# Attention and two feed-forward layers on one core: side work given out one operation at a time, weights converted during layer one, sums in two tiles

## The chip, the cores and the metric

The kernel runs on one core of a Trainium2 chip. A core has a matrix engine (TensorE, PE in the profile), a vector engine (VectorE, DVE), a scalar engine (ScalarE, ACT), GpSimd (POOL) and a sync engine (SP), which here issues nearly all DMAs. Each engine runs its own instructions in order; engines wait for each other through semaphores. The metric is the device time of one launch in microseconds (us).

## The reference

Three functions follow one another, all on 6016 tokens of 256 channels in float32.

```python
qn = q / (np.linalg.norm(q, axis=1, keepdims=True) + 1e-06)      # over the 6016 tokens
kn = k / (np.linalg.norm(k, axis=1, keepdims=True) + 1e-06)
s = kn.transpose(0, 2, 1) @ qn / tau                             # 256 x 256
a = softmax(s);  x = v @ a                                       # 6016 x 256

xn = x / np.sqrt(np.mean(x * x, axis=-1) + 1e-06) * rms_g        # layer one
g = xn @ w_gate;  val = xn @ w_val                               # 256 -> 1536
y = (silu(g) * val) @ w_out                                      # 1536 -> 256

h = y @ w_in                                                     # layer two, 256 -> 2048
out = (h - np.tanh(h)) @ w_out2                                  # 2048 -> 256
```

The weights of both layers are float64 in memory.

## The kernel before

**Numbers.** A float32 factor is split into a high part, rounded to the format in which TensorE takes one pass (`hi_of`, a ScalarE copy), and the rest (`lo_of`, a VectorE subtraction). A product is then three matmuls (`prod`, L132): high with high, low weight with high, high weight with low. The float64 weights are converted by integer operations: one ScalarE copy that scales the upper word (L249, L1010) and three VectorE operations (shift, sign, bits: L253, L256, L260).

**Stages.** Tokens stand in 12 blocks of 512 (the first two 512 and 384), two blocks a pair. (1) Attention reads q and k, accumulates the 256 x 256 scores and the norms, and makes the matrix a. (2) Pair 0 of layer one goes block by block in `gate_block` (L935), while the `converter` turns layer one's weights into high and low parts and saves them to DRAM. (3) Pairs 1 to 5 of layer one use a scheme with 7 products in place of 8 for a 2 x 2 block product. A pair has 6 units (`first_unit`, L799), each with a gate half and a value half; a half is one call of `unit` (L749) with 7 products of 3 matmuls each and 4 fillers. A filler (`fill`) is one product of the second matrix (`acc`), 3 matmuls, of values that an earlier unit left. (4) Layer two runs pairs 0 to 5 with 8 units each (`second_unit`, L1106): 7 products and 8 fillers, 45 matmuls. Pair 0 of layer two has two halves of 448 columns, all others 512.

**A unit.** `unit` uses four PSUM banks X, T, Y, Z. It forms X and T, copies X to Y and T to m5 (ScalarE), adds a product to Y, makes Z = Y + m5 (VectorE), and goes on in X, Y, Z and Y. After each quarter a hook takes a result out: c11 from X, c22 from Y + m5, c12 from Z, c21 from Y. The gate half applies silu; the value half multiplies and splits into `uc` and `ulc`, which the fillers use. What is left over at a unit's end is put in `carried` and runs in the next unit's hooks `early` and `next`.

**Side work.** Everything that is not on this path is a generator wrapped in `Work` (L35), which yields after one operation or a few. `side(n)` (L157) does up to n steps: at each one `Work.clock` goes up, and the first work in the list that can go on takes a step, whatever engine it is for. A yielded number waits for so many clocks, a function until it is true, and "pe" until `between` (L165) between two halves. `force` (L172) and `finish` (L984) run a work's steps one after another until a condition holds. The side works are:
- `first_sums` (L343): the sums of layer one's weights that the scheme needs, six of them, from DRAM into the tile `wraw`;
- `x_operands` (L632): the operands of the next pair. It splits two blocks of v, multiplies by a (x, 12 matmuls a block), squares, takes the mean over channels by a matmul (`ms`), computes 1/rms in a narrow tile with two DRAM trips (`row` to m, `back` to `rs`), multiplies, and then `operands` (L588) forms and splits seven sums;
- `second_weights` (L996): conversion of layer two's weights, 16 items, each loaded into `wraw` (512 KB) and saved to DRAM. At the start of pair 5 `finish(w2_work)` (L1094) runs what is left;
- `second_sums` (L1026): eight times, loads the saved weights into `wraw`, splits them, forms four sums and splits these. It starts when the unit of pair 5 whose weights it replaces is over. `force(s2_work, ...)` (L1182) runs what a unit of layer two still lacks;
- `y_operands` (L1062): in layer two, loads y and forms the operands of the next pair.

## Time and profile before

The median of three runs is 1309.99 us (1307.97 to 1310.6). The profiled execution took 1313.08 us; its span, from the first to the last instruction, is 1311.3 us, and its mean granted TensorE clock 0.95.

| engine | busy, us | share of the span | instructions |
|---|---|---|---|
| TensorE, matmuls | 1175.4 | 90% | 4988 |
| TensorE, weight loads | 943.3 | 72% | 4988 |
| VectorE | 832.9 | 64% | 1402 |
| ScalarE | 690.0 | 53% | 1219 |

Busy time is the sum over the engine's instructions; weight loads overlap matmuls, and the ends of matmuls are modelled. "Idle before" in a row is the time in which the engine had nothing to do before that instruction, and the arrow names what ended it. The clock in a window is the share of full speed that TensorE was granted.

### The profile page before, as it was taken

Reading aid. Unit: us, or ns where it says so; the run is one execution under the profiler, and the core shown is the slowest. Engines: PE = TensorE matmul, PEld = TensorE weight load, DVE = VectorE, ACT = ScalarE, POOL = GpSimd, SP = SyncE. Lnnn points to the kernel's source line nnn. Section 1 sums busy time; section 2 is a strip of 40 time slices with the busy share of each in tenths; the row PEclk is TensorE's granted clock in tenths of the full one; section 3 lists DMA queues with packets and bytes.
Section 4 is the critical chain, followed back from the end, with each engine's and each line's share of the span. In section 5 each row is a group of like instructions: output and inputs, shape, how many; then the busy total and the mean of one; then the engine's idle time right before and its main releaser. Section 6 shows DMA issues by size and latency. Waiting matters only on the chain.

```text
span 1311.3 us, 13924 instructions
## 1 busy us (share of the span) xinstructions
PE 1175.4 (90%) x4988; PEld 943.3 (72%) x4988; DVE 832.9 (64%) x1402; ACT 690.0 (53%) x1219; POOL 0.7 (0%) x6
## 2 busy tenths in 40 slices
PE   9688979995998999999619998879999999999998
PEld 8567867774776777777418777667888888878887
DVE  5777556646556566655636666667667676676765
ACT  5454535554544654654315455446565565665655
POOL 0000000000000000000000000000000000000000
PEclk9788989997999999999859998889999999999999
DMA  9443121102101201111041002101010010100000
GB/s 365 155 160 127 33 65 60 49 4 69 57 25 57 73 25 57 64 33 41 24 132 49 17 23 90 32 25 53 9 51 15 9 49 8 41 17 1 33 0 33
DMA packets 37737, 73.05 MB, mean 56 GB/s; under 512 B 6426, under 2 KB 8218, under 8 KB 37668
## 3 DMA queue, kind: packets, MB, share of 16 engines
q1 hardware_dynamic: 37380, 71.12, 16.0%
q10 hardware_dynamic: 288, 1.05, 0.2%
q8 instruction: 39, 0.64, 0.2%
q14 instruction: 30, 0.25, 0.1%
HBM read 52.45 MB, written 19.70 MB: 55 GB/s over the span
## 4 chain that ended last, share of the span: by engine, by line
PE 55%; DVE 10%; ACT 8%; DMA 3%; issue 2%; SPq 0%; ACTq 0%; DVEq 0%
PE acc L136 23%; PE Yh L136 8%; PE Xh L136 4%; PE Yv L136 4%; PE Yg L136 3%; PE Zh L136 2%; PE Th L136 2%; PE Xv L136 2%; DMA rs<-back 1%; PE Xg L136 1%; ACT hc L124 1%; PE Zv L136 1%; DVE ulc L130 1%; PE x L136 1%; PE Tv L136 1%
## 5 line engine op out<-in xcount | busy, mean ns | idle before, releaser
L136 PE MATMUL acc<-hc,l 128*128 128x512 f32 (+1 forms) x768 | 236.5, 389 | 0.0
L130 DVE TENSOR_TENSOR lc<-wc,hc 128x512 fp32r<-128x512 f32 (+1 forms) x192 | 127.3, 677 | 82.4 <-ACT hc L124 82.4
L136 PEld LDWEIGHTS acc<-hc,l 128*128 128x128 f32 x768 | 146.7, 191 | 27.8
L124 ACT ACTIVATE hc<-wc 128x512 fp32r<-128x512 f32 (+1 forms) x192 | 113.8, 617 | 83.6 <-DVE wc L1114 83.6
L124 ACT ACTIVATE uc<-t 128x512 fp32r<-128x512 f32 x120 | 72.3, 626 | 148.9 <-DVE t L779 148.9
L136 PE MATMUL acc<-lc,l 128*128 128x512 f32 (+1 forms) x384 | 149.1, 388 | 0.0
L130 DVE TENSOR_TENSOR ulc<-t,uc 128x512 fp32r<-128x512 f32 x120 | 79.7, 685 | 12.6 <-ACT uc L124 12.1
L136 PEld LDWEIGHTS acc<-lc,l 128*128 128x128 f32 x384 | 73.2, 191 | 13.7
L136 PE MATMUL Yg<-T2h,sh 128*128 128x512 f32 x30 | 13.3, 444 | 47.7 <-ACT Yg L127 47.5
L1114 DVE TENSOR_TENSOR wc<-Yh,wc 128x512 f32<-128x512 f32 (+1 forms) x48 | 32.7, 680 | 30.8 <-ACT wc L1111 30.8
L1111 ACT ACTIVATE wc<-Xh 128x512 f32<-128x512 f32 (+1 forms) x48 | 28.2, 588 | 44.6 <-PE Xh L136 44.6
L747 DVE TENSOR_TENSOR Zg<-Yg,m5g 128x512 f32<-128x512 f32 x30 | 20.9, 698 | 45.4 <-PE Yg L136 29.5
L782 ACT ACTIVATE t<-t 128x512 f32<-128x512 f32 x30 | 19.0, 632 | 58.0 <-DVE t L747 53.1
L747 DVE TENSOR_TENSOR s<-Yh,m5h 128x512 f32<-128x512 f32 (+1 forms) x48 | 32.6, 680 | 25.5 <-PE Yh L136 25.5
L1111 ACT ACTIVATE wc<-Yh 128x512 f32<-128x512 f32 (+1 forms) x48 | 28.2, 589 | 37.9 <-PE Yh L136 37.9
L408 PE MATMUL S<-q,k 128*128 128x256 f32 x188 | 44.3, 398 | 1.5 <-DMA k<-k_in 1.5
L136 PEld LDWEIGHTS Yg<-T2h,sh 128*128 128x128 f32 x30 | 5.7, 189 | 55.5 <-ACT Yg L127 54.3
L408 PEld LDWEIGHTS S<-q,k 128*128 128x128 f32 x188 | 37.3, 201 | 7.8 <-issue 1.2
L1111 ACT ACTIVATE wc<-s 128x512 f32<-128x512 f32 (+1 forms) x48 | 30.0, 624 | 23.9 <-DVE s L747 23.8
L136 PE MATMUL Th<-T1h,l2s 128*128 128x512 f32 (+1 forms) x96 | 33.3, 422 | 8.8 <-ACT l2s L124 8.3
L1114 DVE TENSOR_TENSOR wc<-Xh,wc 128x512 f32<-128x512 f32 (+1 forms) x48 | 32.5, 676 | 8.8 <-ACT wc L1111 8.4
L136 PE MATMUL Xh<-B11h,l 128*128 128x512 f32 (+1 forms) x96 | 31.1, 396 | 7.7 <-ACT l L124 6.1
(684 smaller groups left out, 3008.7 us busy)
## 6 DMA issues: line engine op xcount, KB each, us to landing
q<-q_in SPq DMA_DIRECT2D x11, 512.0 KB
vraw<-vT_in SPq DMA_DIRECT2D x11, 512.0 KB
y<-r SPq DMA_DIRECT2D x22, 256.0 KB
y<-y SPq DMA_DIRECT2D x20, 256.0 KB
outT<-r SPq DMA_DIRECT2D x20, 256.0 KB
k<-k_in SPq DMA_DIRECT2D x9, 512.0 KB
raw<-w_in_in SPq DMA_DIRECT2D x8, 512.0 KB
l<-y SPq DMA_DIRECT2D x16, 256.0 KB
```

The source lines that it names most:

```text
L124: nc.scalar.activation(out=dst, in_=src, func=AF.Copy, scale=scale)
L130: nc.vector.tensor_sub(out=dst, in0=src, in1=f32(hi))
L136: nc.tensor.matmul(out, a, b, start=start and i == 0, stop=i == 2, skip_group_check=True)
L408: nc.tensor.matmul(S[m][:, :C], kt[:, j, m * P:(m + 1) * P], qt[:, j, :], start=(i == 0 and j == 0), stop=(i == NCH - 1 and j == chunks[i] ...
L747: nc.vector.tensor_add(out=o, in0=a, in1=b)
L782: nc.scalar.activation(out=o, in_=a, func=AF.Silu)
L1111: nc.scalar.activation(out=t[c][:, :n], in_=src, func=AF.Tanh)
L1114: nc.vector.tensor_sub(out=t[c][:, :n], in0=src, in1=t[c][:, :n])
```

## The change

`Work` now says what its next operation is for: "A" (ScalarE), "D" (VectorE) or "pe". `side(a, d)` raises the clock once and gives out up to d VectorE and then up to a ScalarE operations, each to the first work that has one of that kind; a work that has just had a ScalarE operation gets its VectorE operation at a later clock. The table SIDE fixes the numbers at each hook of a unit: 9 and 9 in a unit of layer one, 3 and 3 in one of layer two. `urgent` holds copies out of PSUM that `hurry` puts behind a unit's first two copies.

In `x_operands`, x of pair 1 comes from unsplit v and a in full precision, the low part of v is one operation of 1024 elements, and the two trips of 1/rms through DRAM are issued without clocks between them. `operands` splits two sums at a time. In a unit of layer one the product for c22 and the low part of c21 move from the next gate half's start to the end of the value half, and the high part of c12 the other way; silu of c22 goes behind that of c12. In layer two the low part of c22 moves from `early` to `next`.

`finish(w2_work)` is gone; the conversion of layer two's weights stands behind x in the list in all pairs of layer one, and waits 2 clocks instead of 6 for a load. `second_sums` becomes two works, for the even units in the tile `wraw` and the odd ones in `vraw`; each splits 1024 elements in one operation and loads its next tile right behind its last operation. The core of the diff:

```diff
-SIDES = ((1, 2), (1, 2))
+SIDES = (((1, 1), (1, 2)), ((1, 1), (1, 2)))
...
     def __init__(self, steps):
-        self.steps, self.pe, self.ready, self.done = steps, False, None, False
-
-    def run(self):
+        self.steps, self.kind, self.ready, self.done, self.acted = steps, None, None, False, -1
+        self.advance()
+
+    def advance(self):
         got = next(self.steps, self)
-        self.pe, self.ready = got == "pe", None
+        self.kind = self.ready = None
         if got is self:
             self.done = True
...
-        return not self.done and not self.pe and (self.ready is None or self.ready())
+        else:
+            self.kind = got
+
+    def can(self, kind):
+        while self.ready and self.ready():
+            self.advance()
+        return self.kind == kind and (kind == "A" or self.acted < Work.clock)
+
+    def run(self):
+        if self.kind == "A":
+            self.acted = Work.clock
+        self.advance()
 
...
-    def side(count=1):
-        for _ in range(count):
-            Work.clock += 1
-            w = next((w for w in works if w.can()), None)
-            if w:
-                w.run()
+    def side(a=0, d=0):
+
+        Work.clock += 1
+        for kind, count in (("D", d), ("A", a)):
+            for _ in range(count):
+                w = next((w for w in works if w.can(kind)), None)
+                if w:
+                    w.run()
         works[:] = [w for w in works if not w.done]
...
-        w = next((w for w in works if w.pe), None)
+        w = next((w for w in works if w.can("pe")), None)
         if w:
-            w.pe = False
             w.run()
 
     def force(w, until):
         while not until():
             assert not w.done
             w.run()
+            hurry()
...
-            yield 3
-            for _ in block_sums(y):
-                yield
+            yield 2
+            yield from block_sums(y)
...
+        def split(*parts):
+            hs = []
+            for nm, t in parts:
+                yield "A"
+                hs.append(oh(f"{nm}h"))
+                hi_of(hs[-1][:, :n], t[:, :n])
+            for (nm, t), h in zip(parts, hs):
+                yield "D"
+                l = ol(f"{nm}l")
+                lo_of(l[:, :n], t[:, :n], h[:, :n])
+                out[nm] = (h[:, :n], l[:, :n])
...
+        yield from split(("T1", t1), ("T2", t2))
+        yield "D"
         sub(b12, b22, b12)
-        yield
-        yield from split("T2", t2)
+        yield "D"
         sub(t2, b21, t2)
         yield lambda: last() > 0
-        yield from split("B21", b21)
-        yield from split("T3", b12)
+        yield from split(("B21", b21), ("T3", b12))
         yield lambda: last() > 1
-        yield from split("B22", b22)
-        yield from split("T4", t2)
+        yield from split(("B22", b22), ("T4", t2))
...
-        for t in range(2):
-            b = 2 * p + t
-            if b not in v_raw:
-                load_v(b)
-                yield 4
-            raw = v_raw.pop(b)
-            vh, vl = (act_tile(f"v{x}", 1, f"v{x}{b}", shape=V2) for x in "hl")
+        b0 = 2 * p
+        split, sqs, parts = {}, [[], []], {}
+
+        def split_v(t):
+            raw = v_raw.pop(b0 + t)
+            if p == 1:
+                split[t] = raw
+                return
+            vh, vl = (act_tile(f"v{x}", 1, f"v{x}{b0 + t}", shape=V2) for x in "hl")
             for kk in range(KC):
+                yield "A"
                 hi_of(vh[:, kk], raw[:, kk])
-                yield
-                lo_of(vl[:, kk], raw[:, kk], vh[:, kk])
...
+            yield "D"
+            lo_of(vl, raw, vh)
+            split[t] = vh, vl
+            if b0 + t + 1 < len(blocks):
+                load_v(b0 + t + 1)
...
+                    if p == 1:
+                        x_matmul_full(o, b0 + t, c, kk, split[t])
+                    else:
+                        vh, vl = split[t]
+                        prod(o, a_hl[kk][c], (vh[:, kk], vl[:, kk]), kk == 0)
+                if c == 0:
+                    x_out(t, c, o)
+                else:
+                    urgent.append(lambda: x_out(t, c, o))
...
+        def mean_square(t, later):
+            o = take(f"ms{b0 + t}", 1)
+            for i, x in enumerate(parts[t]):
+                nc.tensor.matmul(o, mean, x, start=i == 0, stop=i == 1)
+
+            def out():
+                copy(sqs[t][1][:1, :], o[:1, :])
+                nc.sync.dma_start(out=row[t:t + 1, :], in_=sqs[t][1][:1, :])
+
+            if later:
+                urgent.append(out)
+            else:
+                out()
+
+        if b0 not in v_raw:
+            load_v(b0)
+            yield 3
+        yield from split_v(0)
+        yield "pe"
+        x_products(0)
+        if p == 1:
+            load_v(b0 + 1)
+        yield from split_v(1)
+        yield from squares(0)
+        yield "pe"
+        mean_square(0, False)
+        x_products(1)
+        if p == 1:
+            load_v(b0 + 2)
+        yield 2
+        yield from squares(1)
+        yield "pe"
+        mean_square(1, True)
+        yield 1
...
-        yield 5
+        yield 4
+        yield "D"
         nc.vector.tensor_scalar_add(out=m, in0=m, scalar1=1e-6)
         for i, op in enumerate(rsqrt_ops(m, y, s)):
+            if i % 3 == 1:
+                yield "D"
             op()
-            if i % 3 == 0:
-                yield
         nc.sync.dma_start(
             out=back.rearrange("t (p g) -> p t g", g=NG), in_=y.rearrange("p (t g) -> p t g", t=2))
-        yield 5
         rs = []
         for t in range(2):
             rs.append(sq_tile(f"rs{p}_{t}"))
             nc.sync.dma_start(out=rs[t], in_=back[t:t + 1, :].to_broadcast([P, BLK]))
-        yield 5
+        yield 4
         for t in range(2):
             for c in range(KC):
+                yield "D"
                 x = B[KC * t + c]
                 nc.vector.tensor_mul(out=x, in0=x, in1=rs[t])
-                yield
...
+        hurry()
...
-            side(2)
+            side(*SIDE["g11"])
 
         def g22(Y, m5):
             t["c22"] = ut(f"t22_{i}")
             add(t["c22"][:, :n], Y, m5)
-            gate("c22", t["c22"][:, :n])
+            side(*SIDE["g22"])
 
         def g12(Z):
             t["c12"] = ut(f"t12_{i}")
             gate("c12", Z)
+            gate("c22", t["c22"][:, :n])
+            side(*SIDE["g12"])
...
-            side(3)
+            side(*SIDE["g21"])
...
+            side(*SIDE["v11"])
...
+            side(*SIDE["v12"])
...
-            high("c12")
+            value("c22", sums["c22"])
+            lower("c21")
 
             def later():
-                lower("c21")
-                value("c22", sums["c22"])
+                high("c12")
                 high("c22")
...
-        between()
-        unit(unit1[i][0], x, n, GAPS1, dict(early=carry(0), next=carry(1), c11=g11, c22=g22, c12=g12, c21=g21),
-             f"g{i}")
-        between()
-
         def early():
             place[1] = (i, 1)
-            side(4)
-
+            side(*SIDE["early"])
+
+        unit(unit1[i][0], x, n, GAPS1, dict(early=carry(0), next=carry(1), c11=g11, c22=g22,
+             c12=g12, c21=g21), f"g{i}")
+        between()
         unit(unit1[i][1], x, n, GAPS1,
-             dict(early=early, next=lambda: None, c11=v11, c22=v22, c12=v12, c21=v21), f"v{i}")
+             dict(early=early, next=lambda: side(*SIDE["next"]), c11=v11, c22=v22, c12=v12, c21=v21), f"v{i}")
         place[1] = (i, 2)
-        side(1)
+
+
+    SIDE = dict(
+        g11=(2, 1), g22=(0, 2), g12=(1, 2), g21=(1, 2), early=(2, 2), next=(0, 0), v11=(2, 0),
+        v12=(1, 0), h_early=(1, 1), h11=(1, 1), h12=(0, 0), h21=(1, 1))
 
...
-                yield 6
+                yield 2
+                yield "A"
                 y = act_tile("wy", 1, f"y{j}{x}", F32, [P, 2 * C])
                 nc.scalar.activation(
                     out=y, in_=raw[:, :, 1].bitcast(F32), func=AF.Copy, scale=REBIAS)
-                yield
+                yield "D"
                 shift(y.bitcast(I32))
-                yield
+                yield "D"
                 sign(y.bitcast(I32), raw[:, :, 1])
-                yield
+                yield "D"
                 bits(y.bitcast(I32), raw[:, :, 0])
                 nc.sync.dma_start(out=saved2[j][x], in_=y)
...
-    def second_sums():
-        for j in range(NU2):
...
-            y = act_tile("wraw", 1, f"l2y{j}", F32, [P, 1, 4 * C])
+    def second_sums(first, tag):
+
+        yield lambda: w2_work.done and place[0] >= NP - 1
+
+        def load(j):
+            y = act_tile(tag, 1, f"l2y{j}", F32, [P, 1, 4 * C])
             for x in range(2):
                 nc.sync.dma_start(out=y[:, 0, 2 * C * x:2 * C * (x + 1)], in_=saved2[j][x])
-            yield 4
-            hs = []
-            for x, tag in enumerate((ta, tb)):
-                t = wpool.tile([P, 4 * C], F32R, tag=tag, name=f"l2{j}{x}")
-                hs.append((t[:, :2 * C], t[:, 2 * C:]))
-                hi_of(hs[x][0], y[:, 0, 2 * C * x:2 * C * (x + 1)])
-                yield
-                lo_of(hs[x][1], y[:, 0, 2 * C * x:2 * C * (x + 1)], hs[x][0])
-                yield
-            for _ in block_sums(y):
-                yield
+            return y
+
+        for j in range(first, NU2, 2):
+            ta, tb, ts, free = HOMES[j]
+            y = load(j)
+            yield 2
+            yield lambda free=free: place[0] > NP - 1 or (
+                place[1][0] > free or place[1] == (free, 2))
+            h, l = (wpool.tile([P, 4 * C], F32R, tag=tag, name=f"l2{j}{x}")
+                    for x, tag in (("h", ta), ("l", tb)))
+            yield "A"
+            hi_of(h, y[:, 0])
+            yield "D"
+            lo_of(l, y[:, 0], h)
+            yield from block_sums(y)
             t = late[0].tile([P, 2 * 3 * P], F32R, tag=ts, name=f"l2s{j}")
             sh, sl = t[:, :3 * P], t[:, 3 * P:]
-            h, l = hs[0]
+            yield "A"
             hi_of(sh, y[:, 0, P:4 * P])
-            yield
+            yield "A"
             hi_of(h[:, :P], y[:, 0, :P])
+            yield "D"
             lo_of(sl, y[:, 0, P:4 * P], sh)
-            yield
+            yield "D"
             lo_of(l[:, :P], y[:, 0, :P], h[:, :P])
-            unit2[j], out2[j] = seven(h, l, sh, sl), hs[1]
-            yield
+            unit2[j], out2[j] = seven(h, l, sh, sl), (h[:, 2 * C:], l[:, 2 * C:])
...
-        yield 5
+        yield 2
...
     w2_work = Work(second_weights())
-    s2_work = Work(second_sums())
+    s2_works = [Work(second_sums(i, tag)) for i, tag in enumerate(("wraw", "vraw"))]
...
         else:
-            finish(w2_work)
             x_work = Work(y_operands(0, progress(p, NU1), x_next))
-        works[:] = ([sums_work] if not sums_work.done else []) + [x_work]
-        works.append(w2_work if p + 1 < NP else s2_work)
+        works[:] = [w for w in (sums_work, x_work, w2_work, *s2_works) if not w.done]
...
-            side(1)
+            side(*SIDE["h11"])
...
             def later():
                 lower("c12")
                 high("c22")
-                lower("c22")
 
             carried[0].append(later)
-            side(1)
+            carried[1].append(lambda: lower("c22"))
+            side(*SIDE["h21"])
...
-            side(2)
+            side(*SIDE["h_early"])
...
         for j in range(NU2):
-            force(s2_work, lambda: unit2[j] is not None)
+            force(s2_works[j % 2], lambda: unit2[j] is not None)
             second_unit(j, x, n, A)
```

## Rows read from the trace of the kernel before

**Rows 1.** Table of windows, by stage: us, busy (instructions) by engine, clock, DMA share, GB/s.
```profile
185.20:193.48 8.28, 1.57 (x6) 1.06 (x5) 4.67 (x10) 1.52 (x3) 0.00 (x0) 0.78 0.39 128
193.48:205.93 12.45, 10.39 (x35) 7.80 (x33) 9.25 (x17) 6.55 (x12) 0.00 (x0) 0.73 0.00 1
205.93:310.45 104.52, 91.90 (x393) 71.91 (x392) 61.40 (x111) 51.27 (x94) 0.00 (x0) 0.96 0.16 52
310.45:423.27 112.82, 103.75 (x424) 79.07 (x425) 70.63 (x122) 56.13 (x101) 0.00 (x0) 0.97 0.14 45
423.27:532.37 109.10, 101.67 (x425) 79.41 (x424) 67.11 (x116) 56.39 (x102) 0.00 (x0) 0.98 0.15 46
641.44:690.51 49.07, 10.66 (x35) 8.20 (x33) 19.09 (x32) 11.78 (x21) 0.00 (x0) 0.58 0.32 104
690.51:775.75 85.24, 84.36 (x364) 67.30 (x363) 53.15 (x91) 43.51 (x81) 0.00 (x0) 1.00 0.09 32
775.75:885.18 109.43, 90.66 (x361) 74.97 (x360) 70.08 (x136) 55.25 (x112) 0.00 (x0) 0.88 0.14 46
969.93:1053.09 83.16, 82.59 (x362) 67.12 (x361) 58.59 (x91) 51.43 (x92) 0.00 (x0) 1.00 0.08 26
```

**Rows 2.** Table of windows, single half-units of layer one and units of layer two.
```profile
490.40:497.88 7.48, 7.48 (x34) 6.20 (x33) 3.89 (x8) 1.99 (x4) 0.00 (x0) 1.00 0.04 2
373.51:381.15 7.64, 7.64 (x34) 6.04 (x33) 5.86 (x17) 4.71 (x9) 0.00 (x0) 1.00 0.18 43
532.37:544.22 11.85, 9.48 (x34) 7.03 (x33) 8.72 (x15) 8.23 (x16) 0.00 (x0) 0.86 0.00 1
554.75:564.20 9.45, 8.66 (x36) 6.35 (x35) 3.79 (x6) 5.63 (x11) 0.00 (x0) 1.00 0.33 112
506.55:515.90 9.35, 7.80 (x34) 6.12 (x33) 4.25 (x7) 1.98 (x4) 0.00 (x0) 1.00 0.63 194
515.90:524.15 8.25, 7.79 (x34) 6.05 (x33) 6.40 (x11) 4.72 (x9) 0.00 (x0) 1.00 0.00 0
775.75:787.90 12.15, 10.34 (x47) 8.30 (x45) 8.65 (x16) 7.48 (x16) 0.00 (x0) 1.00 0.08 31
824.90:839.65 14.75, 11.66 (x45) 9.49 (x45) 9.48 (x19) 6.92 (x15) 0.00 (x0) 0.88 0.12 37
1022.44:1032.64 10.20, 10.20 (x47) 8.45 (x45) 6.56 (x10) 5.80 (x11) 0.00 (x0) 1.00 0.01 2
```

**Rows 3.** Waits from 641.44 to 690.51: waiter, releaser, total, times, longest.
```profile
PE Yg L136 <- ACT Yg L127: 38.4, 1, 38.4
ACT y L1010 <- DMA raw<-w_out_in: 19.5, 3, 7.3
```

**Rows 4.** Timeline, one load of raw weights: start, duration, engine, line, operation.
```profile
649.44 0.39 SPq L1005 DMA_DIRECT2D raw<-w_out_in  x1
653.30 0.66 ACT L1010 ACTIVATE y<-raw 128x512 f32<-128x512 f32 x1 [7.28 <-DMA raw<-w_out_in]
```

**Rows 5.** Timeline and chain of waits around a unit of layer two's pair 0.
```profile
827.97 1.34 PE L136 MATMUL Th<-T1h,l2s 128*128 128x448 f32 x2 [1.67 <-ACT l2s L124]
...
832.45 1.22 PE acc L136 x6
```

**Rows 6.** Timeline, the two DRAM trips of 1/rms at pair 1's end.
```profile
302.57 0.36 SPq L690 DMA_DIRECT2D back<-naryp  x1
...
309.04 0.69 DVE L701 TENSOR_TENSOR x_0g<-x_0g,rs 128x512 f32<-128x512 f32 x1 [6.49 <-DMA rs<-back]
```

**Rows 7.** Timeline, x of pair 0 in full precision.
```profile
64.46 4.35 PE L535 MATMUL x<-vraw,a 128*128 128x512 f32 x10 [0.38 <-DVE a L515]
```

**Rows 8.** Timeline, two neighbours on VectorE.
```profile
409.78 0.70 DVE L747 TENSOR_TENSOR Zg<-Yg,m5g 128x512 f32<-128x512 f32 x1 [0.81 <-ACT uc L124]
410.39 0.68 DVE L130 TENSOR_TENSOR ulc<-t,uc 128x512 fp32r<-128x512 f32 x1
```

More of the change, by code (lines that the diff above doesn't have):

```diff
@@ L655, in x_operands, with x_products @@
+        def x_products(t):
             for c in range(KC):
-                xs.append(take(f"x{b}_{c}", c))
+                o = take(f"x{b0 + t}_{c}", c)
                 for kk in range(KC):
-                    prod(xs[c], a_hl[kk][c], (vh[:, kk], vl[:, kk]), kk == 0)
-            sqs = []
-            for c in range(KC):
-                sqs.append(sq_tile(f"sq{b}_{c}"))
-                nc.scalar.activation(out=sqs[c], in_=xs[c], func=AF.Square)
-                B.append(ox(f"x{b}_{c}g"))
-                nc.scalar.activation(
-                    out=B[-1], in_=xs[c], func=AF.Copy, scale=g_t[:, c:c + 1])
@@ L666, in x_operands @@
-            yield 2
-            nc.vector.tensor_add(out=sqs[0], in0=sqs[0], in1=sqs[1])
-            yield
-            sh, sl = sq_part(f"sh{b}"), sq_part(f"sl{b}")
-            hi_of(sh, sqs[0])
-            yield
-            lo_of(sl, sqs[0], sh)
-            yield "pe"
-            o = take(f"ms{b}", 1)
-            nc.tensor.matmul(o, mean, sh, start=True, stop=False)
-            nc.tensor.matmul(o, mean, sl, start=False, stop=True)
-            copy(sqs[1][:1, :], o[:1, :])
-            nc.sync.dma_start(out=row[t:t + 1, :], in_=sqs[1][:1, :])
@@ L679, in x_operands, with squares @@
-            yield
-        yield 4
+                    if p == 1:
[7 more added lines that the diff above has]
+                    urgent.append(lambda: x_out(t, c, o))
+        def squares(t):
+            yield "D"
+            add(sqs[t][0], sqs[t][0], sqs[t][1])
+            parts[t] = sq_part(f"sh{b0 + t}"), sq_part(f"sl{b0 + t}")
+            yield "A"
+            hi_of(parts[t][0], sqs[t][0])
+            yield "D"
+            lo_of(parts[t][1], sqs[t][0], parts[t][0])
@@ L953, in gate_block @@
             fill()
-        side(sides[1])
+        side(*sides[1])
         between()
+        hurry()
     works.append(converter)
@@ L984, in finish @@
     def finish(w):
-        force(w, lambda: w.done)
+        while not w.done:
+            w.run()
+            hurry()
     finish(x_work)
@@ L1141, in h12 @@
             rest("c12", Z)
+            side(*SIDE["h12"])
         def h21(Y):
@@ L1175, in attn_moe_kernel @@
         n = REST // 2 if p == 0 else BLK
-        works[:] = [] if s2_work.done else [s2_work]
+        works[:] = [w for w in s2_works if not w.done]
         if p + 1 < NP:
```

75 lines of the change are left out of this document (35 added, 40 removed).

## The prediction

> **What bounds the kernel now.** I read the table of windows first, one window for each stage [rows 1]. TensorE is the bound: in the stage 969.93 to 1053.09 it is busy for 82.59 of 83.16 us at full clock, VectorE for 59 and ScalarE for 51. So the question in every other stage is how far TensorE stays behind its own pace. That pace comes from two windows without a gap [rows 2]: half a unit of layer one (33 matmuls; the count takes in one that began before) in 7.48 us, a unit of layer two (45) in 10.20, both 0.2267 us for a matmul of 512 columns. A pair of layer one should so take 12 x 7.48 = 89.8 us, and 6.3 for 28 matmuls of the next pair's x and mean squares: 96.1. Pair 1 takes 117.0 (12.45 + 104.52), pair 2 112.8, pairs 3 and 4 109.1 each: 20.9, 16.7, 13.0 and 13.0 us lost, together 63.6. Pair 5 prepares no x: 134.3 (49.07 + 85.24) against 89.8, so 44.5 lost. Layer two's pair 0 has 448 columns; six such matmuls take 1.22 us [rows 5], the pair at pace 8 x 45 x 0.2033 = 73.2, and it takes 109.4: 36.2 lost. A later pair loses 1.6 (83.16 against 8 x 10.20). Ahead of pair 1 TensorE does almost nothing from 185.20 to 193.48.
>
> What ends these losses stands in the lists of waits and the timeline. In pair 5 one matmul waits 38.4 us for the copy of Yg on ScalarE; that copy stands behind the conversions of layer two's weights, three of which alone waited 19.5 us for their load [rows 3]: `finish(w2_work)` runs the rest of that work in one piece. A load takes from its issue at 649.44 to 653.30 [rows 4], and with a single buffer the next is issued only when VectorE has read the last. In layer two's pair 0 the matmuls wait for the sums that `force` runs ahead of a unit, 1.67 us for one l2s [rows 5]; such a unit takes 14.75 us instead of 9.15 [rows 2].
>
> **The change, part by part.** I walked through the steps of each side work by hand against the slots that each unit gives (9 on ScalarE and 9 on VectorE in a unit of layer one, 3 and 3 in layer two), to see in which unit each step falls.
>
> *Weights of layer two.* There are 16 items of one ScalarE and three VectorE operations; before the change six conversions are left for pair 5. Pairs 1 to 4 give 4 x 54 = 216 VectorE slots; x takes 25 in each (100), the last three sums of layer one 18, the weights 48: 166. With the two clocks of waiting for each load the last item falls into unit 2 of pair 4. Nothing is left to finish at pair 5, and the 49.07 us of its first half-unit become an ordinary one: 41.6 less. The operations don't vanish (0.66 us for the conversion [rows 4]); they lie beside matmuls.
>
> *Sums of layer two.* With two tiles and wider operations four of the eight are ready at the end of pair 5, and the fifth lacks two operations, which unit 0 gives. Units 5 and 7 still force two and five operations; after the 1.67 us now [rows 5] I give these 1 and 2 us. The first unit takes 12.15 us now [rows 2], 3 over pace, and the four late splits of x still come there: 3 again. The other five units get 3 together. So 9 are lost instead of 36.2: 27 less. Their price in pair 5: up to seven VectorE operations stand in a gate half, and the sum c22 has to be done before the matmul that writes Y again. A half with 11 VectorE operations takes 8.25 us, one with 17 (the many small ones of the root among them) 7.64 [rows 2]. I take 0.5 us for each of six units, 3 for the start of the pair: 6 lost in place of all 44.5, so 38.5 less in pair 5, the 41.6 included.
>
> *x of the next pair.* What it costs now is in [rows 2]: a first half-unit of 11.85 us instead of 7.48 (ten operations forced in a row), 9.45 for a half with a mean square (35 matmuls, 7.93 at pace), 9.35 where VectorE stands waiting for the row of 1/rms. After the change all but six operations are given out inside pairs 2 to 4 (twelve remain in pair 1, whose first slots go to layer one's sums). ScalarE empties x's banks at once, and the bank of the second mean square is not asked for again until later in the value half. The root's two DMAs, 6.5 us from 302.57 to 309.04 [rows 6], are issued together; the first use stands behind more than a half-unit, some 13 us at pace. `value c22` and `lower c21` move from the start of the gate half to the end of the value half and leave VectorE free for Z. I take 6.5 lost in a pair: 2.5 at its start, 2 for gates full of side work, 2 for x and mean squares; 8 in pair 2 because of the twelve. That makes 27.5 in place of 58.6 (63.6 without 5.0 of the first half-unit, which belongs to the next part): 31 less.
>
> *Pair 0.* All operands of pair 1 now fit into its loop, so of the 8.28 us ahead of pair 1 [rows 1] only the two small matmuls stay: 7 less. The half-unit behind it runs at 0.73 of the clock and loses 5.0; without the idle time ahead I take 1: 4 less. Against that, x of pair 1 comes from 8 products in full precision instead of 24 of rounded parts: five took 4.35 us [rows 7], so 7.0 against 5.4, 1.5 more. And the second block of v is loaded into the buffer that the first has just left: 3.9 us, as for the raw weights of that size [rows 4], against about 3 us of matmuls in between; 1 more with the mean square's chain beside it. 8.5 less.
>
> *The rest of layer two* stays at TensorE's pace. `lower c22` goes behind Z, and five operations are forced at a pair's end instead of four: 0, between 3 less and 5 more over five pairs.
>
> [...] On VectorE one operation starts 0.61 us behind another that lasts 0.70 [rows 8], so neighbours overlap, and I price a side operation at 0.61. [...]
>
> Sum against the profiled execution: 8.5 + 31 + 38.5 + 27 = 105, a span of 1206.3 instead of 1311.3. That run took 1313.08, 1.8 more than its span, and the median of the runs shown is 1309.99, 3.1 below it: 1313.1 - 105 - 3.1 = **1205 us**. Bounds: with every stage named at pace 11 + 58.6 + 44.5 + 36.2 = 150 would go (1160). If the 41.6 go and half of the rest, 73 (1237).
>
> **Rivals.**
> *Loads come late.* ScalarE's conversion stands two clocks behind its load. Where these are from g12 to early, TensorE has 15 matmuls or 3.4 us to do, and the load takes 3.9 from an issue that itself waits for the last reader. Behind the conversion stand c11's operations. A half in which VectorE waited 5.4 us lost 1.9 [rows 2]; 16 of these are 30: 1235. For it: the short distance. Against: a wait of 1 to 2 us is less than the 3.5 that were hidden there. The Trainium skill ("TensorE: Matmul & The Clock Gate", "Architectural detail: the array is 16× 32×32, not 1× 128×128") calls ScalarE and VectorE strict FIFO; by that rule nothing overtakes such a wait, and the 38.4 us of the copy agree.
> *Sums late after all.* If a step that I place in layer one is forced (the change then doesn't do what it says), the sums start later and layer two's pair 0 forces as now: the 27 stay, 1232. For: x has precedence in every slot. Against: 50 of 216 slots stay empty by my count.
> *Better hidden.* If the slots are as fine as they look, the 2 + 2 us in each of five pairs and the 3 + 2 of layer two's units go too: 25 less, 1180.
> *Slower.* Side work pushes VectorE behind TensorE: its operations stand in one queue ahead of the sums on which the next matmul waits. With all 210 exposed at 0.61 us, pairs 1 to 5 take 128 more, 1333. It decides from the point where own operations and slots of a half exceed 7.48 us; four own ones leave room for eight. Against: the fullest gate has seven, and 17 operations passed in 7.64 us.
>
> **How the numbers follow.** The forecast gets 0.62 (its own spread 1188 to 1222), better hidden 0.13, loads late 0.10, sums late 0.10, slower 0.03, several small shortfalls 0.02. The range 1176 to 1236 leaves out the slower case and the tail of the better one. This kernel's measurement can tell about 0.2% (2.6 us) from no change; all cases but one lie far below: faster 0.96, same 0.01, slower 0.03.
>
> **What would show it.** No wait of a matmul above 3 us from 190 on; pairs 2 to 4 at 100 to 106 us, pair 5 at 93 to 99, layer two's pair 0 at 78 to 86 with short waits for l2s ahead of units 5 and 7 only, later pairs at 83 to 85, and the clock at 0.98 or more from pair 1 on. It would be wrong if conversions wait for raw by more than 3 us, if gate halves take more than 9 us, or if x's operations still come in a row of ten at a pair's start.

## The result and the profile after

The changed kernel takes 1200.87 us (median of 4 runs, 1199.98 to 1202.87) against 1309.35 for the kernel before: 0.9174 of its time, 95% interval 0.9158 to 0.919. The forecast was 1205, range 1176 to 1236. The profiled execution took 1201.24 us with a span of 1199.3; before, 1313.08 and 1311.3.

The page of the kernel after, busy time by engine, and the chain that ended last by engine (PE 55% before):

```profile
PE 1143.6 (95%) x4980; PEld 931.9 (78%) x4980; DVE 826.0 (69%) x1382; ACT 690.9 (58%) x1207; POOL 0.7 (0%) x6
...
PE 78%; DVE 8%; DMA 6%; ACT 5%; issue 2%; SPq 0%; ACTq 0%; DVEq 0%
```

The table of windows after, by stage, as [rows 1]: the first half-unit of pair 1, the rest of pair 1, pairs 2, 3 and 4, the first half-unit of pair 5 and its rest, layer two's pairs 0 and 1. A line has start and end, length, then busy time and instructions of TensorE, its weight loads, VectorE, ScalarE and GpSimd, the clock, the DMA engines' share and GB/s.

```profile
188.35:196.66 8.31, 7.51 (x33) 6.04 (x34) 5.14 (x9) 5.70 (x11) 0.00 (x0) 1.00 0.01 2
196.66:293.85 97.19, 90.51 (x392) 72.36 (x391) 63.11 (x112) 52.11 (x92) 0.00 (x0) 0.99 0.19 59
293.85:401.75 107.90, 102.35 (x424) 81.11 (x425) 73.87 (x126) 60.20 (x107) 0.00 (x0) 0.95 0.21 61
401.75:503.13 101.38, 98.57 (x426) 78.52 (x425) 69.61 (x120) 58.28 (x104) 0.00 (x0) 1.00 0.21 66
503.13:602.99 99.86, 98.13 (x426) 78.58 (x425) 68.08 (x117) 57.34 (x102) 0.00 (x0) 1.00 0.17 51
602.99:611.19 8.20, 7.95 (x34) 6.04 (x33) 7.15 (x13) 6.14 (x12) 0.00 (x0) 1.00 0.45 141
611.19:694.69 83.50, 83.49 (x364) 67.35 (x363) 59.40 (x105) 48.11 (x87) 0.00 (x0) 1.00 0.14 49
694.69:773.67 78.98, 75.05 (x362) 67.29 (x360) 60.32 (x112) 50.72 (x99) 0.00 (x0) 1.00 0.11 37
773.67:859.86 86.19, 83.54 (x362) 68.57 (x360) 61.07 (x95) 52.45 (x94) 0.00 (x0) 0.98 0.08 26
```

Pair 5 is at TensorE's pace (91.70 us in all, 134.31 before), and no stage of the table but pair 2 has a lower clock than 0.98. Pair 2 starts with a stall. Windows of the kernel after: the last half-unit of pair 1 and the first of pair 2, the first of pair 3, gate 4 of pairs 3 and 4, a value half of pair 5, the last unit of layer two's pair 0 and the first of its pair 1.

```profile
281.59:293.85 12.26, 7.64 (x34) 6.01 (x32) 8.17 (x14) 3.80 (x7) 0.00 (x0) 0.90 0.39 107
293.85:311.23 17.38, 14.75 (x46) 10.71 (x47) 13.24 (x21) 10.92 (x20) 0.00 (x0) 0.68 0.12 36
401.75:412.76 11.01, 10.76 (x47) 8.21 (x45) 9.08 (x15) 9.20 (x17) 0.00 (x0) 1.00 0.16 50
471.34:480.34 9.00, 7.92 (x34) 6.04 (x33) 6.14 (x11) 5.76 (x11) 0.00 (x0) 1.00 0.08 31
572.58:580.23 7.65, 7.65 (x35) 6.12 (x33) 6.16 (x11) 5.46 (x10) 0.00 (x0) 1.00 0.00 0
641.54:649.30 7.76, 7.76 (x34) 6.12 (x33) 4.67 (x10) 2.53 (x6) 0.00 (x0) 1.00 0.17 62
762.62:773.67 11.05, 9.65 (x47) 8.37 (x45) 7.74 (x15) 6.93 (x15) 0.00 (x0) 1.00 0.01 1
773.67:788.01 14.34, 11.82 (x46) 9.53 (x45) 11.67 (x19) 8.90 (x18) 0.00 (x0) 0.88 0.30 105
```

Waits of TensorE from 188 to 774, and of the other two from 188 on (waiter, releaser, total, times, longest):

```profile
PE Yg L147 <- ACT Yg L138: 5.6, 7, 1.5
PE Xg L147 <- ACT B11h L135: 4.6, 1, 4.6
...
PE Yv L147 <- DVE Zv L166: 1.6, 1, 1.6
...
PE Yg L147 <- DVE t L166: 1.1, 3, 0.4
```

```profile
DVE Zv L166 <- ACT x_1g L689: 43.8, 8, 7.1
...
ACT y L1086 <- DMA raw<-w_in_in: 11.1, 4, 4.5
ACT y L1086 <- DMA raw<-w_out_in: 10.4, 5, 4.1
```

The 38.4 us of [rows 3] are gone: no wait of that kind above 1.5 us is left. The longest wait of a matmul is 4.6 us, for B11h at the start of pair 2. VectorE's new wait of 43.8 us, for the copies of x out of bank Z, costs next to nothing: only 1.6 us of TensorE's time wait for Zv behind it.

### The profile page after: what moved, and what is told of

Read it like the earlier page. It is cut to its first block, busy times and chain, and to the rows that moved or that the text cites. A ratio compares the mean times of both kernels' runs of the same rounds, so it can differ in the third digit from the quotient of the medians.

```text
span 1199.3 us, 13912 instructions
## 1 busy us (share of the span) xinstructions
PE 1143.6 (95%) x4980; PEld 931.9 (78%) x4980; DVE 826.0 (69%) x1382; ACT 690.9 (58%) x1207; POOL 0.7 (0%) x6
## 4 chain that ended last, share of the span: by engine, by line
PE 78%; DVE 8%; DMA 6%; ACT 5%; issue 2%; SPq 0%; ACTq 0%; DVEq 0%
PE acc L147 32%; PE Yh L147 8%; PE Yg L147 5%; PE Yv L147 5%; PE Xh L147 5%; PE Xv L147 3%; PE Xg L147 3%; PE Zh L147 3%; PE Th L147 2%; PE x L147 2%; DMA k<-k_in 2%; PE g L147 2%; PE v L147 2%; PE Zv L147 2%; PE Tv L147 2%
## 5 line engine op out<-in xcount | busy, mean ns | idle before, releaser
L166 DVE TENSOR_TENSOR Zv<-Yv,m5v 128x512 f32<-128x512 f32 x30 | 21.0, 699 | 77.6 <-ACT x_1g L689 43.8
L166 DVE TENSOR_TENSOR Zh<-Yh,m5h 128x512 f32<-128x512 f32 (+1 forms) x48 | 33.0, 687 | 45.6 <-PE Yh L147 41.5
L1188 DVE TENSOR_TENSOR wc<-s,wc 128x512 f32<-128x512 f32 (+1 forms) x48 | 32.7, 681 | 9.4 <-ACT wc L1185 9.4
L438 DVE TENSOR_TENSOR acc<-acc,sq 128x1024 f32<-128x1024 f32 (+1 forms) x24 | 24.0, 1023 | 18.0 <-ACT sq L463 17.6
L147 PE MATMUL Yh<-T2h,l2s 128*128 128x512 f32 (+1 forms) x96 | 30.5, 399 | 4.9 <-ACT Yh L138 4.2
L847 ACT ACTIVATE t<-Zg 128x512 f32<-128x512 f32 x30 | 17.9, 596 | 28.4 <-PE Zg L147 28.4
L166 DVE TENSOR_TENSOR c<-Yv,m5v 128x512 f32<-128x512 f32 x30 | 20.7, 691 | 18.9 <-PE Yv L147 17.3
L1188 DVE TENSOR_TENSOR wc<-Zh,wc 128x512 f32<-128x512 f32 (+1 forms) x48 | 32.3, 672 | 0.0
L147 PE MATMUL Th<-T1h,l2s 128*128 128x512 f32 (+1 forms) x96 | 29.8, 389 | 2.5 <-ACT l2s L135 1.3
```

The costliest lines, as they stand in the source:

```text
L147: nc.tensor.matmul(out, a, b, start=start and i == 0, stop=i == 2, skip_group_check=True)
L166: nc.vector.tensor_add(out=o, in0=a, in1=b)
L438: nc.vector.tensor_add(out=out, in0=a, in1=b)
L847: nc.scalar.activation(out=o, in_=a, func=AF.Silu)
L1188: nc.vector.tensor_sub(out=t[c][:, :n], in0=src, in1=t[c][:, :n])
```

## The experiments

Differences in microseconds are against the changed kernel's median of 1200.87. For the five kernels from `x_first` to `comb_trips` they are worked out from the ratios, against its second measurement: 1202.58, ratio 0.9189 (interval 0.9177 to 0.9202). That one was foretold so:

> The changed kernel unaltered, as the ground for the other kernels of this call: 0.917 to 0.918 of the kernel before, 1200 to 1202.

**Hold back the last conversions.**

```
+                if (j, x) == (5, 0):
+                    yield lambda: place[0] >= NP - 1
...
             x_work = Work(y_operands(0, progress(p, NU1), x_next))
+            finish(w2_work)
```

> The last six of the sixteen conversions of layer two's weights are held back until pair 5 and run in one piece at its start, as in the kernel before. Theory (the forecast's largest term: what goes away is the row of loads that ScalarE's queue waits for, ahead of the copy of Yg): the first half-unit of pair 5 grows from 8.2 us back to about 49, 41 more, and the places in pairs 2 to 4 where a conversion waited for its load give back 2 to 4, so 1238 to 1241 instead of 1201, with one matmul wait of 35 to 40 us for the copy of Yg. Rival (pair 5 is short because VectorE and ScalarE are ordered otherwise, the row itself is mostly hidden): under 15 us more, no wait above 10 us.

1243.00, ratio 0.9495 (0.9481 to 0.9509): 42.1 more. The first half-unit of pair 5, and its waits from 600 to 652.6:

```profile
600.47:652.60 52.13, 9.94 (x35) 7.68 (x34) 18.15 (x31) 10.13 (x18) 0.00 (x0) 0.57 0.38 124
```

```profile
PE Yg L147 <- ACT Yg L138: 42.2, 1, 42.2
...
ACT y L1088 <- DMA raw<-w_in_in: 19.7, 3, 7.5
ACT y L1088 <- DMA raw<-w_out_in: 18.3, 3, 6.3
```

Of the 42.2 us in which TensorE waits for the copy of Yg, ScalarE waits 38.0 for six loads. Pairs 3 and 4, with fewer conversions, give back 2.6 (gate 4 of pair 3, counted from 0: 7.64 instead of 9.00), so that pair 5 starts 2.5 earlier. The theory's sum holds: 43.9 less 2.5 are the 41.5 by which the span grows.

**One tile for layer two's sums.**

```
-    s2_works = [Work(second_sums(i, tag)) for i, tag in enumerate(("wraw", "vraw"))]
+    s2_works = [Work(second_sums(0, "wraw"))]      # j in range(NU2), step 1
```

> The sums of layer two are one side work in a single tile again; the wider operations, their slots and the order stay. Following the steps by hand, four of the eight are still ready at the end of pair 5, and in layer two's pair 0 the fifth row is as now (2 operations ahead of unit 5), but eight operations are forced ahead of unit 6 and eight ahead of unit 7 instead of none and five. Theory (a forced row costs, the second tile takes away rows): a row of eight behind a load costs the 5.6 us of such a unit in the kernel before, two of them 11, less the 1.9 of unit 7 now and some 3 at the start of pair 1, whose operands come earlier: 6 more, 1207, all of it in units 6 and 7. Rival one (the two tiles are what brought the 27 us of this stage): 20 to 27 more. Rival two (only the width of the operations counts): 0 to 2 more.

1210.39, ratio 0.9247 (0.9233 to 0.926): 9.5 more. Units 6 and 7 of layer two's pair 0:

```profile
757.27:770.23 12.96, 9.93 (x47) 8.31 (x45) 10.10 (x19) 7.24 (x15) 0.00 (x0) 1.00 0.19 61
770.23:785.77 15.54, 12.63 (x47) 10.57 (x45) 10.14 (x19) 6.41 (x14) 0.00 (x0) 0.78 0.00 1
```

Two forced rows add 8.3 here, and the first unit of pair 1 gets 3.7 back (10.63 instead of 14.34): near the theory's 9 (11 less 1.9) and 3. What it missed are 2.3 us in pair 5, where the single work's steps fall into other halves; 1.3 more were lost ahead of pair 5, where the two kernels don't differ. So of the 30.5 us of this stage the second tile carries about 8. That the rest comes with the wider operations and the earlier start is argued: no run takes those back.

**More work for VectorE.** One operation more behind each side operation, then behind every second one:

```
                 if w:
                     w.run()
+                    if kind == "D" and 1 <= place[0] < NP:      # dose_half: every second time
+                        nc.vector.tensor_sub(out=extra, in0=extra, in1=extra)
...
```

> One more VectorE operation (128 x 512, result unused) stands behind each side operation of VectorE given out in pairs 1 to 5: 181 of them at 0.61 us, 110 us of VectorE's time. This asks how far the kernel is from the case in which VectorE bounds it. If VectorE's free time of a whole unit can be used (the order within it doesn't matter): 19 more, the sum over units of what exceeds TensorE's time. If each half-unit has to hold its own (the forecast's rule: own operations and slots against 7.48 us): 58 more, mostly in gate halves with seven slots. If side operations stand in front of what the next matmul needs wherever they are: 110 more. Value halves should stay at 7.5 us in the second and third case.

1273.05, ratio 0.9733 (0.971 to 0.9756): 72 more, 0.40 us for each of 181. This lies between two theories, and the place was foretold wrongly: value halves, which should have stayed at 7.5, paid 40 us of it and gate halves 32. (The next expectation puts nearly all of it into value halves; that is a misreading.) The side operations given out at the end of a gate run in the value half. A value half of pair 5:

```profile
701.53:711.81 10.28, 7.78 (x34) 6.12 (x33) 7.87 (x16) 2.52 (x6) 0.00 (x0) 1.00 0.12 48
```

> The extra VectorE operation stands behind every second side operation only (about 90 in pairs 1 to 5). With all 181 the kernel took 72 us more, 0.40 for each, and nearly all of it in value halves, whose VectorE time rose from about 5.0 to 8.9 us. If VectorE has room up to TensorE's 7.5 us and costs only from there (the rule from which the forecast judged the slower case): three more in a unit are 1.9 us in a value half that has 2.5 free, so 5 to 15 more, 1206 to 1216, in the fullest halves alone. If every added operation costs its share wherever it is: half of 72, 36 more, 1237.

1234.44, ratio 0.943 (0.9403 to 0.9457): 34 more, 0.37 for each of 91. So there is no free room up to a point, as I had assumed; as far as two doses show, the price is a line through zero. A value half and a gate half of pair 5, and TensorE's waits from 193 to 720:

```profile
668.28:677.59 9.31, 7.77 (x34) 6.12 (x33) 6.25 (x13) 2.52 (x6) 0.00 (x0) 1.00 0.14 53
677.59:685.70 8.11, 7.78 (x35) 6.12 (x33) 6.59 (x12) 6.06 (x10) 0.00 (x0) 1.00 0.02 3
```

```profile
PE Yg L147 <- DVE t L166: 8.3, 16, 1.0
PE Yv L147 <- DVE Zv L166: 7.3, 5, 3.2
...
PE Yg L147 <- ACT Yg L138: 6.1, 6, 2.0
...
PE Yv L147 <- ACT Yv L138: 5.2, 6, 1.5
```

VectorE is busy for 6.25 us in that value half of 9.31, so it is not full. Over pairs 1 to 5 TensorE's waits grow by 22 us; 16 of these are for results of VectorE itself, whose queue now holds the added operations. In a gate the operation stands ahead of c22's sum, which frees bank Y (1.1 us in 3 waits without the additions, 8.3 in 16 with them). Another 5 us are for the copy of Yv: in the value half the timeline shows ScalarE's rounding of l2s waiting 2.50 us for VectorE's block sums, and the copy of Yv behind it. To test the latter:

```
-        g11=(2, 1), g22=(0, 2), g12=(1, 2), g21=(1, 2), early=(2, 2), next=(0, 0), v11=(2, 0),
+        g11=(2, 1), g22=(0, 2), g12=(1, 2), g21=(0, 2), early=(3, 2), next=(0, 0), v11=(2, 0),
```

> The kernel with an extra VectorE operation behind every second side operation (34 us more than the changed kernel), in which the one ScalarE slot at the end of a gate half is given behind the value half's copies of Y and m5 instead of ahead of them. Theory (in a value half the price is not VectorE's own time but an order of two queues: ScalarE's side operation stands ahead of the copy of Yv and itself waits for VectorE's side operations, 2.5 us for one rounding of l2s; TensorE then waits for that copy): the value halves of pair 5, 8.5 to 9.3 us, fall to 7.5 to 7.9, and 6 to 10 of the 34 us go: 1224 to 1228; the gate halves keep their 0.6, since there TensorE waits for c22's sum, behind an extra operation of VectorE itself. Rival (VectorE is late by itself, the sum for Z comes late however ScalarE is ordered): value halves stay above 8.3 and the time within 3 us of 1234.

1233.25, ratio 0.9428 (0.941 to 0.9445): the same time. The same two halves, and the wait:

```profile
673.14:680.62 7.48, 7.48 (x35) 6.19 (x33) 6.25 (x13) 2.71 (x6) 0.00 (x0) 1.00 0.18 62
680.62:688.72 8.10, 7.78 (x35) 6.12 (x33) 6.58 (x12) 6.06 (x10) 0.00 (x0) 1.00 0.01 3
```

```profile
PE Yg L147 <- ACT Yg L138: 9.3, 6, 2.3
PE Yv L147 <- DVE Zv L166: 9.1, 6, 3.2
...
PE Yv L147 <- ACT Yv L138: 0.7, 1, 0.7
```

At its place the theory is shown: with the same 6.25 us of VectorE's time the value half is at TensorE's pace, the waits for Yv's copy fall from 5.2 to 0.7, and pair 5 gives back 6.1. Four of its five long value halves fall to 7.48; the fifth stays at 8.86, with VectorE busy for 8.15 us and Zv late, as the rival has it. And in the pairs that prepare x the shifted ScalarE slot makes other things late (Yg's copy and Zv wait 5 us more), and the sum is nothing. The total I foretold is wrong.

The Trainium skill's "TensorE: Matmul & The Clock Gate", section "Architectural detail: the array is 16× 32×32, not 1× 128×128", calls ScalarE and VectorE strict FIFO. The value half agrees: 9.31 us with the rounding ahead of the copy, 7.48 with it behind.

**x of pair 1 by rounded parts.** The four branches on `p == 1` in `x_operands` are taken out.

> x of pair 1 is made from 24 products of rounded parts as in the kernel before, not from 8 in full precision; so each of its two blocks of v is rounded and split first. By the steps, twelve of its operations are then left over and forced at the end of pair 0 (none now) and fourteen instead of twenty-four at the end of pair 1. Theory (what counts is whether a row of operations is left at a pair's end): 5 to 8 more ahead of and in the first half-unit of pair 1, 1.6 less for the products, 4 to 8 less at the start of pair 2: between 5 less and 4 more in all, but the start of pair 1 late by 4 to 7. Rival (the full precision itself is the gain, and rows of a dozen cost little): the start of pair 1 within 2 us of now.

1201.09, ratio 0.9181 (0.9165 to 0.9197): the same. The first half-unit of pair 1, and of pair 2:

```profile
190.34:207.11 16.77, 13.28 (x47) 9.96 (x45) 11.45 (x21) 9.74 (x18) 0.00 (x0) 0.80 0.18 50
...
295.28:310.74 15.46, 12.30 (x46) 9.38 (x45) 11.32 (x19) 9.03 (x17) 0.00 (x0) 0.89 0.29 82
```

Pair 1 starts 2.0 us later and its first half-unit takes 8.5 more (16.77 against 8.31): 10.4 behind at that point. By the start of pair 2's second half-unit all of it is back: 4.4 within pair 1, and 6.5 about the start of pair 2, where 23.1 us stand against 29.6. Layer one's last sums are done about a unit earlier here (at 237 against 245 us), and by the steps a shorter row is left at the end of pair 1. In the changed kernel the full precision buys its start with that later row.

**x ahead of the sums in layer one.**

```
-        works[:] = [w for w in (sums_work, x_work, w2_work, *s2_works) if not w.done]
+        works[:] = [w for w in (x_work, sums_work, w2_work, *s2_works) if not w.done]
```

> In layer one's pairs x's operations are taken ahead of the sums' in each slot, not behind them. By the steps, the row of 24 operations that is left over at the end of pair 1 shrinks to the seven of the other pairs; in exchange two operations of layer one's sums are forced ahead of unit 4 and six ahead of unit 5. Theory (rows at a pair's start are what is left of the loss there): the last half-unit of pair 1 and the first of pair 2, 12.3 and 17.4 us now, become 7.5 and 11.0 as in pair 3, 11 less; the forced sums give 2 to 4 back: 7 to 9 less, 1192 to 1194. Rival (a forced sum costs a full wait of its own: a load from DRAM and ten operations in front of a unit, 5.6 us each as in layer two before): 0 to 3 less.

1199.27, ratio 0.9153 (0.9137 to 0.917): 4.7 less (3.3 by the medians). The last gate half of pair 1 and the first half-unit of pair 2 (7.48 us lie between them):

```profile
276.52:288.88 12.36, 9.55 (x34) 6.95 (x33) 8.20 (x15) 6.48 (x12) 0.00 (x0) 0.86 0.14 44
...
296.36:307.36 11.00, 10.75 (x46) 8.22 (x45) 9.09 (x15) 9.20 (x17) 0.00 (x0) 1.00 0.15 48
```

The row goes for the foretold 11 (29.64 to 18.48). The forced sums ahead of units 4 and 5 take 6.2, not 2 to 4. So the place of the gain is the theory's, its size lies between both.

**The two moved operations.**

```
-            value("c22", sums["c22"])
-            lower("c21")
+            high("c12")
...
-                high("c12")
+                lower("c21")
+                value("c22", sums["c22"])
```

> The two operations of VectorE that the change moved from the start of the next gate half to the end of the value half (the value product of c22, the lower part of c21) stand at the start of the next gate half again, and the rounding of c12 at the end of the value half, as before the change; all else stays. Theory (they stood ahead of the sum Z on which the gate's matmuls wait, and gates are the fuller halves): 0.6 to 1.3 us in each of 30 gate halves, 18 to 39 more, 1219 to 1240. Rival (VectorE catches up within the gate, the place doesn't matter): within 3 us of now.

1205.76, ratio 0.9211 (0.9198 to 0.9223): 3 more, and the two intervals touch. Gate 3 of pair 3 (7.48 in the changed kernel):

```profile
456.05:463.96 7.91, 7.77 (x34) 6.12 (x33) 6.10 (x20) 4.81 (x9) 0.00 (x0) 1.00 0.00 0
```

The theory falls: most gate halves don't change, ten of 30 take 0.4 to 0.5 more, 4.5 in all. The rival's sum holds, though not its reason: the place does matter a little, and the first half-unit of pair 2 hides part of it by taking 2.7 less (14.62, at a clock of 0.88 instead of 0.68).

**The trips of 1/rms on another queue.** In the kernel after, SP issues a raw load behind the trip, in value half 3 of pair 2; its conversion starts 6.4 us after that issue:

```profile
362.11 0.36 SPq L758 DMA_DIRECT2D back<-naryp  x1
363.74 0.81 SPq L763 DMA_DIRECT2D rs<-back  x2
...
365.13 0.38 SPq L1080 DMA_DIRECT2D raw<-w_in_in  x1
...
371.55 0.66 ACT L1086 ACTIVATE y<-raw 128x512 f32<-128x512 f32 x1 [4.46 <-DMA raw<-w_in_in]
```

The edit: the loads of `m` and `rs` and the store of `back` use `nc.gpsimd.dma_start`.

> The DRAM trips of 1/rms of the next pair's x (the row of mean squares back in, the roots out, two broadcasts) are issued from GpSimd's queue in place of SP's; the loads of raw weights stay on SP's, where they stood behind the trips. Theory (a raw load whose conversion waits 4.1 to 4.5 us in gate 4 of pairs 2 and 3, and in the last half-unit of pair 1, is late because it is issued behind the trip and shares the transfer's time with the two broadcasts): it is issued 1.5 to 2.5 us sooner, that wait falls to 2 or less, and gate 4 goes from 9.0 to 9.4 us to about 7.7: 3 to 5 less, 1197 to 1199. Rival one (the transfer is the limit: 1.28 MB together at about 400 GB/s): the order changes, the wait stays within 1 us, no change. Rival two (GpSimd's queue issues later than SP's): the norms wait for the broadcasts instead, 2 to 6 more.

1195.85, ratio 0.9129 (0.9115 to 0.9144): 7.9 less. The same load and gate 4 of pair 2, and the waits for raw:

```profile
360.66 0.38 SPq L1080 DMA_DIRECT2D raw<-w_in_in  x1
...
365.70 0.68 ACT L1086 ACTIVATE y<-raw 128x512 f32<-128x512 f32 x1 [2.29 <-DMA raw<-w_in_in]
```

```profile
365.93:373.57 7.64, 7.64 (x35) 6.12 (x34) 6.15 (x11) 5.70 (x11) 0.00 (x0) 1.00 0.08 30
```

```profile
ACT y L1086 <- DMA raw<-w_out_in: 8.8, 5, 2.4
ACT y L1086 <- DMA raw<-w_in_in: 7.2, 4, 2.6
```

The conversion now starts 5.0 us after the issue, and its wait falls from 4.46 to 2.29. Gate 4 of pairs 2 and 3 goes from 9.38 and 9.00 to 7.64 and 7.63, and the half-units about the start of pair 2 from 29.64 to 26.31: 6.4 in all. The theory holds at these places, with more gain in the whole than foretold; the waits stay at 2.3 to 2.6 instead of 2 or less. The traces separate its two parts. Counted from the start of their half, the three loads that waited over 4 us are issued 1.5, 0.8 and 1.6 us sooner. The time from issue to conversion falls in one of them alone (6.42 to 5.04; the others 5.29 to 5.33 and 5.20 to 5.15). So most of it is the earlier issue. `comb_trips` against `comb` repeats the step: gate 4 of pairs 2 to 4 takes 7.63 instead of 9.04 to 9.46.

The Trainium skill ("DMA: Bandwidth & Descriptors", "Rules for kernel authors") says that spreading transfers over several issuing engines only saves issue time. The traces agree in two of the three loads, which take as long as before and only start sooner. Part of what is saved is a wait: SP stood 1.2 us for `back` to land before it issued the two loads of `rs`, and the raw load stood behind them.

**Both together.** `comb` is x first with a fourth slot per unit in layer two (`h12=(1, 1)`); `comb_trips` adds the trips.

> x ahead of the sums in layer one, and in layer two a fourth slot per unit on each engine, behind the operations of c12 (the changed kernel gives none there). By the steps, nothing is forced any more ahead of a unit of layer two's pair 0 (two and five operations now), and the operands of its pair 1 leave six operations at the end in place of twelve. Theory (rows cost, single operations between TensorE's steps don't): 7 to 9 less from layer one; in layer two units 5 and 7 go from 10.45 and 11.05 to 9.3, and pair 1's first unit from 14.3 to 10.6: 6 less; together 1186 to 1189. Rival (VectorE is near its limit there: 13 operations in a unit of 9.12 us take 7.0 to 8.0 of it, and four more slots push the sum for Z back): units of layer two's pair 0 grow by 0.5 us each, and 1191 to 1196 comes out.

1196.60 (1192.81 to 1200.38), ratio 0.9141 (0.912 to 0.9161), 6.3 less, just above the rival's range. In the profile units 5 and 7 of layer two's pair 0 do fall to 9.33 and 9.12 and pair 1's first unit to 10.12, but the second units of pairs 0 to 4 grow by 0.5 to 0.95. So neither theory has the whole: the rows go as foretold, and the slots have a price, in other units than the rival says.

> The kernel with x ahead of the sums and the fourth slot in layer two's units, with the trips of 1/rms issued from GpSimd's queue. Theory: 3 to 5 less than that kernel, whose median was 1196.6 (0.914 of the kernel before), so 0.910 to 0.912. Rival: no difference (0.914), or later norms, 0.916 to 0.919.

1192.58 (1191.08 to 1193.86), ratio 0.91 (0.9086 to 0.9114): 11.6 less than the changed kernel. It is the fastest version measured, and the step from `comb` is in the theory's range.

## Why the prediction was right

By its terms, forecast and measured in the two profiled executions:

| term | forecast | measured |
|---|---|---|
| ahead of pair 1, and its first half-unit | 8.5 | 9.3 (5.1 + 4.1) |
| pairs 1 to 4 without that half-unit | 31 | 29.2 (435.5 to 406.3) |
| pair 5 | 38.5 | 42.6 (134.3 to 91.7) |
| layer two, pair 0 | 27 | 30.5 (109.4 to 79.0) |
| rest | 0 | 0.5 |
| sum | 105 | 112.0 |

How far the causes are shown differs. Taking back parts of the change shows about 50 of the 112 us: the conversions (41.5) and the second tile (9.5 in the whole kernel). For pairs 1 to 4 the trace shows what went, but no run takes back the new way of giving out side work: from the second half-unit of pair 1 to the end of pair 4 TensorE stands idle for 16.8 us instead of 36.3, and its matmuls are busy for 9.6 less. The waits that shrank most are those for Zv (7.9 to 1.6) and for B11h at a pair's start (10.0 to 4.6). That the finer slots did this is argued.

**Pair 5** was right in mechanism and in its largest number: holding six conversions back costs 41.5 us of the span, the forecast's step 41.6. Too dear were the 6 us that I booked for seven side operations in a gate: pair 5 loses 1.9 against pace. The `dose` runs show how narrow that is. The side operations that are there cost almost nothing, and the next ones 0.37 to 0.40 us each.

**Layer two's pair 0** loses 5.8 us instead of 9: forced operations stood ahead of units 5 and 7 only, as foretold (10.45 and 11.05). The two tiles are about 8 us of the stage, shown; the rest is argued, as said above.

**Pairs 1 to 4** have the right sum by two errors against each other. Pairs 3 and 4 lose 5.3 and 3.8, less than the 6.5 booked. Pair 1 loses 8.6 behind its first half-unit instead of 6.5, and pair 2 loses 11.8 instead of 8: at 107.9 it lies outside the 100 to 106. By my steps I had placed layer one's last sums about a unit too early, so that 24 operations of x were left at the end of pair 1, not twelve; the trace shows 22 in a row from 292.45 on. `x_first` shows that this row is worth 11 us at its place and that moving it brings less than half, since the sums are forced instead. The two moved operations, which I counted among the reasons, are worth some 3 us (`moves_undone`).

**Pair 0** came out near its term, 9.3 for 8.5, and at its place by the mechanism named. What I had not seen is that this is no gain in the whole: `x_parts` has the same time without the full precision. The gain is one of place, paid later, for the larger part by the row just named.

**The claims.** "No wait above 3 us" failed once (4.6). All three signs that I had named for a wrong forecast appeared, each at a few places: three conversions waited 4.1 to 4.5 us for raw, gate 4 of pair 2 took 9.38 us, and x's operations came in a row at the start of pair 2. As proof they were too strict: two of the waits cost 1.4 to 1.7 us each, the row 11. Pair 2's clock (0.95) missed the 0.98; pairs 4 and 5 and most later pairs came out below their ranges (99.9, 91.7 and 82.4 to 82.8), the first later pair above (86.2). "Loads come late" is thus a real mechanism at a few places and worth 6 to 8 us with what follows from it, not 30.

**The slower case** I judged by a rule that is not enough: VectorE's own time against 7.48 us. A half-unit with 6.25 us of VectorE's time took 9.31, or 7.48 in another order; there two queues that wait for each other in a fixed order decide. In most of the waits that the additions made longer it is VectorE's queue alone: what the added operation stands ahead of. My count of 210 side operations on VectorE in pairs 1 to 5 was high as well, since 181 were given out in slots. The case didn't come. That its chance of 0.03 was too low is my reading of a price of 0.37 to 0.40 us from the first addition on; no run can show a chance.

**Better hidden** has a slip in its sum: the 4 us are booked in four pairs, not in five, so 21 less, not 25. The measured 112 lies between the forecast's 105 and that case.

## What to carry to other kernels

Price side work by what stands behind it in each queue, not by the engine's free time: add a dummy operation to every slot and half as many, and see whether the price starts at zero. An edit's gain at its own place is no gain until the next stages have been read, as x of pair 1 shows: 10.4 us there, nothing in the whole. Ask of each transfer what its issuing queue waits for ahead of it.

## What the runs showed of the hardware

A stall of TensorE costs more than its wait. The half-units on both sides of the start of pair 2 take 29.6 us; those about the start of pair 3 take 18.5 (7.50 and 11.01). Of the 11.1 between them, 7.0 are time in which TensorE stands idle, and 4.1 are longer matmul time, nearly all of it in the first half-unit of pair 2: after the waits of 4.6 and 1.1 us the granted clock of the half-unit was 0.68, a mean between the two levels of 1.2 and 2.4 GHz, and 46 matmul records kept TensorE busy for 14.75 us, where 47 took 10.76 at 1.00 at 401.75.

The price is not a fixed one. With the trips on the other queue the wait at the same place is 3.1 us, and the half-unit behind it:

```profile
291.99:307.53 15.54, 12.91 (x46) 9.36 (x47) 13.16 (x21) 10.93 (x20) 0.00 (x0) 0.81 0.12 36
```
